# Holding back the first pieces of a layer until the last attention products are issued

## The chip, the cores and the metric

The kernel runs as one program on one core of a Trainium2 chip. The metric is the device time of one launch in microseconds (us). Three runs of the kernel before took 715.47 us in the median (715.36 to 720.8). Times are told from the start of the profiled span.

## The reference

Three blocks follow each other; q, k, v are 2 batches x 8 heads x 1152 positions x 64.

```python
q_pool = q.reshape(B, H, S // 2, 2, D).mean(axis=3)          # 576 queries a head
attn   = softmax(scale * q_pool @ k.T) ; y = attn @ v        # 16 heads
x = y as 1152 tokens x 512
h = x @ w_in                                                  # 512 x 2048
g = (a0 + a1*h + a2*h*h + a3*h**3) / (1 + |b0|*|h| + |b1|*h*h + 1e-6)
x = g @ w_out                                                 # 2048 x 512
xn = x / rms(x) * rms_g
out = (silu(xn @ w_gate) * (xn @ w_val)) @ w_out2             # 512 x 1536, 1536 x 512
```

## The kernel before, in words

**Precision.** Products of the two layers are made from pairs: a float32 number is kept as a rounded high part and the rest (`x_hi`, `x_lo`, `win_hi`, `win_lo`), and each product is three matmuls, high by high, low by high, high by low (function `three`, line 525).

**Attention.** The 16 heads are worked in 8 pairs; each pair has 9 row tiles. For a tile, TensorE makes the scores (L783), VectorE the row maximum (L812), ScalarE the exponential (L818), TensorE the transposes (L834, the last of them apart), and ScalarE or VectorE copies them out (L866, L869) into `pt`. When a head's tiles are there, 18 matmuls (9 key blocks x 2 halves, L938) make the products with the values in `av`. For a pair the row sums are inverted (L912, L913), spread by GpSimd into `rx` (L921, L923) and transposed (L985; for the last rows L971, the operation `o_rT`, copied out as `rxh` by L975). `av` is copied into `xt` (L616, L619), divided (L989 on VectorE for the first 512 columns, L994 on GpSimd for the rest), and split into `x_hi` and `x_lo` (L616 or L619, and L632).

**First layer.** Its 2048 hidden columns are 16 units of 128 (numbered from 0 here), its 1152 tokens three thirds of 384 columns. A unit's projection (L525 into `hid`) is 12 pieces: a third by one of four 128-row blocks of x, three matmuls a piece. Block 3 of the second and the last third needs the last pair of heads; the other 10 pieces of a unit don't. For units 0 and 1 (`FINE`) each piece is an operation of its own, and the rational function behind it is worked a third at a time; later units are worked whole. That function is a chain between ScalarE (ACT) and VectorE (DVE): ACT `m_u` (L1125) and `m_p` (L1128), DVE `m_q` (L1141), `m_p` twice (L1131, L1134), ACT L1144, L1147, L1153, DVE L1162, L1156, L1165, then ACT `g_hi` (L1173) and mostly GpSimd `g_lo` (L1176). L1134 is the last that reads `hid`. `hid` has two buffers, so that unit 2 waits for unit 0's L1134 and unit 3 for unit 1's. The second product (L525 into `accp`, also two buffers) sums the units of a group in PSUM; ACT (L1229) or DVE (L1231) takes each sum out into `acc`.

**Weights.** They are split on the chip as well. Those that have no room yet are made during attention and stored back to memory ("spill": ACT L175 and L215, DVE L180 and L223, GpSimd L219, the rounding L230 on ACT or L232 on GpSimd, GpSimd L236, then a DMA, L241), and fetched later (L248). `wc` has two buffers, `spill` two.

**What sets the order.** The program is recorded as operations (`Op`) with an engine (or several to choose from), a cost, a due time (`key`), the operations it waits for and its buffers. `order` walks through them with its own clock and issues, engine by engine, the ready operation that is due first. Each engine then takes its instructions strictly in that order. The due time of a unit's pieces is `key + 1960 * c` for third c; `attention` links the matmuls of the tiles and the products with values in a list `seq`, but the last head's 18 and `o_rT` stand behind no list. The first call of `order` covers attention and the projections of units 0 and 1, the second all the rest.

Of the kernel before, what the change touches and what calls it, by code (L numbers as in the profile page):

```python
# [19 lines left out]
def attention_moe_moe2_kernel(  # L20
# [425 lines left out]
    def cost(eng, n):  # L446
        return {PE: 0.45 * n, DVE: 75 + 1.04 * n, ACT: 120 + 0.834 * n, POOL: 150 + 2.13 * n}[eng]

    wop = {}
# [48 lines left out]
    xop = {}  # L498
    xread = {}

    def project_ops(w, u, key, free=(), ps=None):
        ps = ps or Buf("hid")
        if w == "in" and u in FINE or w in ("gate", "val") and u == 0:
            parts = [(c, [kk]) for c in range(NC) for kk in range(KC)]
        else:
            parts = [(c, range(KC)) for c in range(NC)]
        done = {}
        for c, kks in parts:
            before = done.setdefault(c, [])
            before.append(Op(  # L510
                PE, cost(PE, 3 * len(kks) * CW), key + 1960 * c,
                lambda c=c, kks=kks: project(w, u, c, kks),
                [wop.get((w, u)), *free, *before[-1:], *xread.get((w, u, c), ()), *(o for kk in kks for o in xop.get((c, kk), ()))],
                [ps, *wbuf[w, u]],
            ))
        return ps, done
# [72 lines left out]
    NP = len(heads) // 2  # L589
# [16 lines left out]
    NT = len(TILES)  # L606

    QW = SQ // 2
    TS = 3100
# [287 lines left out]
    def pair_ops(pr):  # L897
# [31 lines left out]
        for h in range(2):  # L929
            ab = Buf("av")  # L930
            last = None
            key = base + LAST[h] * TS + 9500
# [35 lines left out]
            if h == 1:  # L968

                def f_rT():  # L970
                    nc.tensor.transpose(e["av", 1][:, 384:512], e["rx"][:, NFULL].rearrange("p a d -> p (a d)"), ident)  # L971

                def f_rxh():
                    e["rxh"] = T("rxh", [128, 128])
                    nc.scalar.activation(e["rxh"], e["av", 1][:, 384:512], AF.Copy)  # L975

                o_rT = Op(PE, 120, key - 200, f_rT, [o_rx, last], [ab, rxb])
                o_rxh = Op(ACT, 170, key - 100, f_rxh, [o_rT], [ab, rhb])

        pb = Buf("prep")  # L980
# [35 lines left out]

    WARM = 9

    tile_pe, av_ops = {}, []
    AV2 = 5  # L1020

    def attention():
# [27 lines left out]
    early_h = {}  # L1050
# [9 lines left out]
            xop[c, kk] = [x_op[b, kk] for b in range(B) if b * SQ < (c + 1) * CW and (b + 1) * SQ > c * CW]  # L1060
    for u in FINE:
        free = [o for g in range(3) for o in lo_op[NP * NT - 2 + u, g]]
        early_h[u] = project_ops("in", u, (NP * NT + 6 * u) * TS, free)
    order(80)
    scope.pop()
    inner.close()
# [459 lines left out]
```

## Time and profile before

| | us |
|---|---|
| median of 3 runs (lowest, highest) | 715.47 (715.36, 720.8) |
| profiled execution | 718.36 |
| its span, first to last instruction | 716.6 |
| TensorE busy in the span | 689.0 (96%) |
| DVE busy, ACT busy, GpSimd (POOL) busy | 546.1, 397.6, 258.6 |
| attention's part, to the last head's products | about 277 |

The profiled execution took 1.8 us more than its span, and 2.9 us more than the median of the runs. A busy TensorE is not one at its peak: matmuls overlap, a record of 0.33 us is followed by the next after 0.17 us, and the granted clock says at which of its two levels, 1.2 or 2.4 GHz, the engine ran. The mean granted clock of the span is 0.99 of full speed.

### The profile page before, as it was taken

Reading aid. Unit: us, or ns where it says so; the run is one execution under the profiler, and the core shown is the slowest. Engines: PE = TensorE matmul, PEld = TensorE weight load, DVE = VectorE, ACT = ScalarE, POOL = GpSimd, SP = SyncE. Lnnn points to the kernel's source line nnn. Section 1 sums busy time; section 2 is a strip of 40 time slices with the busy share of each in tenths; the row PEclk is TensorE's granted clock in tenths of the full one; section 3 lists DMA queues with packets and bytes.
Section 4 is the critical chain, followed back from the end, with each engine's and each line's share of the span. In section 5 each row is a group of like instructions: output and inputs, shape, how many; then the busy total and the mean of one; then the engine's idle time right before and its main releaser. Section 6 shows DMA issues by size and latency. Waiting matters only on the chain.

```text
span 716.6 us, 13077 instructions
## 1 busy us (share of the span) xinstructions
PE 689.0 (96%) x5257; PEld 596.5 (83%) x5257; DVE 546.1 (76%) x721; ACT 397.6 (55%) x630; POOL 258.6 (36%) x240
## 2 busy tenths in 40 slices
PE   7999999999999999899999999998999999999997
PEld 6666666667666677899999999997999899989996
DVE  5599998989898885997996967957768156845844
ACT  4568776878877875977755655344334232402210
POOL 3022334656654465312221323255345033403500
PEclk9799999999999999999999999999999999999999
DMA  6443434765554535214105104000225112420103
GB/s 209 113 133 119 124 96 156 223 192 180 202 168 143 190 120 202 93 59 146 60 30 171 36 2 149 28 29 0 89 89 148 60 59 83 125 89 29 59 1 132
DMA packets 53900, 77.66 MB, mean 108 GB/s; under 512 B 6480, under 2 KB 36176, under 8 KB 53840
## 3 DMA queue, kind: packets, MB, share of 16 engines
q1 hardware_dynamic: 53840, 76.83, 33.3%
q8 instruction: 41, 0.67, 0.4%
q14 instruction: 19, 0.16, 0.1%
HBM read 62.40 MB, written 14.42 MB: 107 GB/s over the span
## 4 chain that ended last, share of the span: by engine, by line
PE 81%; DVE 12%; ACT 4%; issue 2%; DMA 0%; SPq 0%; DVEq 0%; ACTq 0%
PE hid L525 32%; PE accp L525 23%; PE hid L783 9%; PE av L938 9%; PE hid L834 5%; DVE nm L812 2%; DVE pt L869 2%; ACT p L818 2%; PE prep L732 2%; DVE acc L1324 1%; DVE xt L619 1%; DVE m_q L1141 1%; PE prep L985 1%; DVE wc L184 1%; DVE x_lo L1334 0%
## 5 line engine op out<-in xcount | busy, mean ns | idle before, releaser
L525 PE MATMUL hid<-x_hi,win_hi 128*128 128x384 f32 x480 | 162.3, 338 | 3.6 <-DVE m_p L1134 1.4
L525 PE MATMUL hid<-x_lo,win_hi 128*128 128x384 f32 x480 | 161.2, 336 | 0.6 <-DVE x_lo L1334 0.6
L525 PE MATMUL hid<-x_hi,win_lo 128*128 128x384 f32 x480 | 161.1, 336 | 0.0
L818 ACT ACTIVATE p<-hid,nm 128x1152 f32<-128x1152 f32 x72 | 87.9, 1222 | 28.2 <-DVE nm L812 28.0
L812 DVE TENSOR_REDUCE nm<-hid 128x1 f32<-128x1152 f32 x72 | 94.9, 1353 | 10.2 <-PE hid L783 8.9
L525 PEld LDWEIGHTS hid<-x_hi,win_hi 128*128 128x128 f32 x480 | 90.7, 189 | 6.7 <-issue 3.5
L783 PE MATMUL hid<-kT,qT 64*128 64x256 f32 (+3 forms) x800 | 95.2, 379 | 0.8 <-DVE pt L869 0.4
L1176 POOL TENSOR_TENSOR g_lo<-m_p,g_hi 128x1152 fp32r<-128x1152 f32 (+1 forms) x20 | 44.5, 2233 | 135.2 <-ACT g_hi L1173 96.8
L525 PEld LDWEIGHTS hid<-x_lo,win_hi 128*128 128x128 f32 x480 | 90.6, 189 | 1.8 <-DVE x_lo L1334 0.9
L525 PEld LDWEIGHTS hid<-x_hi,win_lo 128*128 128x128 f32 x480 | 90.5, 189 | 0.0
L834 PEld LDWEIGHTS hid<-ident,p 64*128 64x128 f32 x1296 | 53.6, 141 | 37.7 <-ACT p L818 12.3
L834 PE MATMUL hid<-ident,p 64*128 64x64 f32 x1296 | 68.5, 232 | 12.2 <-ACT p L818 7.0
L783 PEld LDWEIGHTS hid<-kT,qT 64*128 64x128 f32 (+1 forms) x800 | 70.5, 182 | 9.0 <-DVE pt L869 1.3
L938 PE MATMUL av<-pt,vn 128*64 128x288 f32 x576 | 76.7, 411 | 0.0
L866 ACT ACTIVATE pt<-hid 128x512 f32<-128x512 f32 (+2 forms) x145 | 59.7, 449 | 29.8 <-PE hid L834 29.3
L525 PE MATMUL accp<-g_hi,wout_hi 128*128 128x384 f32 x192 | 64.8, 337 | 3.0 <-ACT acc L1229 1.8
L525 PE MATMUL accp<-g_hi,wout_lo 128*128 128x384 f32 x192 | 64.2, 334 | 0.0
L525 PE MATMUL accp<-g_lo,wout_hi 128*128 128x384 f32 x192 | 64.2, 334 | 0.0
L938 PEld LDWEIGHTS av<-pt,vn 128*64 128x64 f32 x576 | 38.7, 136 | 27.1 <-issue 3.4
L175 ACT ACTIVATE wc<-wraw 128x512 f32<-128x512 f32 x68 | 45.4, 671 | 26.5 <-POOL win_lo L208 14.7
L869 DVE COPY pt<-hid 128x512 f32<-128x512 f32 (+1 forms) x79 | 47.6, 608 | 16.4 <-PE hid L834 14.9
L203 POOL TENSOR_SCALAR win_hi<-wc 128x512 fp32r<-128x512 f32 x22 | 15.2, 691 | 99.8 <-PE hid L525 90.8
(120 smaller groups left out, 1236.2 us busy)
## 6 DMA issues: line engine op xcount, KB each, us to landing
wraw<-in_moe_w_out_dram SPq DMA_DIRECT2D x28, 512.0 KB, 3.4
far<-spill SPq DMA_DIRECT2D x23, 512.0 KB, 3.3
wraw<-in_moe_w_in_dram SPq DMA_DIRECT2D x16, 512.0 KB, 3.8
wraw<-in_moe_w_gate_dram SPq DMA_DIRECT2D x12, 512.0 KB, 3.8
wraw<-in_moe_w_val_dram SPq DMA_DIRECT2D x12, 512.0 KB, 4.2
kn<-in_k_dram SPq DMA_DIRECT2D x16, 288.0 KB, 3.9
vn<-in_v_dram SPq DMA_DIRECT2D x16, 288.0 KB, 3.1
qn<-in_q_dram SPq DMA_DIRECT2D x16, 256.0 KB, 3.3
```

The lines of the kernel that those rows point to most:

```text
L175: nc.scalar.activation(c.bitcast(F32), wt["raw", n][:, :, 1].bitcast(F32), AF.Abs, scale=2.0**-112)
L203: eng.tensor_scalar(hi, w_float(n), 1.0, 1.0, op0=ALU.mult, op1=ALU.mult)
L525: ins = nc.tensor.matmul(dst, lhsT=a[x], rhs=b[y], start=first and i == 0 and p == 0, stop=last and i == n - 1 and p == 2,)
L732: seen(nc.tensor.transpose(ps[:, at:at + 128], src, ident))
L783: ins = nc.tensor.matmul(ps[to, j, c:c + x1 - x0], lhsT=qT[2 * pr + h][rows, c0:c0 + to.stop - to.start], rhs=kT[2 * pr + h][rows, x0:x1], ...
L812: nc.vector.tensor_reduce(out=e["nm"], in_=scores(), op=ALU.max, axis=AX.X, negate=True)
L818: nc.scalar.activation(e["p"], scores(), AF.Exp, bias=e["nm"], scale=1.0, accum_out=sums[pr][:, t:t + 1])
L834: ins = nc.tensor.transpose(ps[:, g, c:c + 64], e["p"][rows, 128 * j:128 * j + 128], ident[rows, rows])
L866: return nc.scalar.activation(to, src, AF.Copy)
L869: return nc.vector.tensor_copy(to, src)
L938: nc.tensor.matmul(e["av", h][64 * c:64 * c + 64, 0:QW], lhsT=v_tile[2 * pr + h][:, KEYS[kt], :], rhs=pt[pr, h][:, kt, c * QW:(c + 1) * QW ...
L1176: eng.tensor_sub(g_(1), p_(), g_(0).bitcast(F32))
```

## The change

All but the first two pieces of unit 0, and all pieces of unit 1, get one more operation to wait for: `o_rT` of the last pair, the matmul behind the last head's products with the values. No instruction's work changes. The wait is one in the recorded order alone (TensorE runs in order, so it needs no semaphore). Since the due times and costs are walked through anew, the places of other operations behind it move as well.

```diff
-    def project_ops(w, u, key, free=(), ps=None):
+    def project_ops(w, u, key, free=(), ps=None, behind=(), ahead=0):
...
-        for c, kks in parts:
+        for n, (c, kks) in enumerate(parts):
...
-                [wop.get((w, u)), *free, *before[-1:], *xread.get((w, u, c), ()), *(o for kk in kks for o in xop.get((c, kk), ()))],
+                [wop.get((w, u)), *free, *(behind if n >= ahead else ()), *before[-1:], *xread.get((w, u, c), ()), *(o for kk in kks for o in xop.get((c, kk), ()))],
...
                 o_rT = Op(PE, 120, key - 200, f_rT, [o_rx, last], [ab, rxb])
+                av_last[:] = [o_rT]
...
-    tile_pe, av_ops = {}, []
+    tile_pe, av_ops, av_last = {}, [], []
...
-        early_h[u] = project_ops("in", u, (NP * NT + 6 * u) * TS, free)
+        early_h[u] = project_ops("in", u, (NP * NT + 6 * u) * TS, free, None, av_last, 0 if u else 2)
```

Behind line 976 the changed kernel's lines have a number one higher (L1125 is L1126 there). Three places show what stands where now.

**TensorE (PE) at the end of attention.** Three L525 rows are one piece; L834 is the last row tile's transposes, L938 the last head's products, L971 `o_rT`. Before, the tenth piece and what follows:

```order
L525 MATMUL hid<-x_hi,win_hi 128x384
L525 MATMUL hid<-x_lo,win_hi 128x384
L525 MATMUL hid<-x_hi,win_lo 128x384
L985 MATMUL prep<-ident,rx 128x128 x4
L834 MATMUL hid<-ident,p 128x64
L938 MATMUL av<-pt,vn 64x288 x18
L971 MATMUL av<-ident,rx 128x128
```

and now, from the transposes:

```order
L834 MATMUL hid<-ident,p 128x64 x35
L525 MATMUL hid<-x_hi,win_hi 128x384
L525 MATMUL hid<-x_lo,win_hi 128x384
L525 MATMUL hid<-x_hi,win_lo 128x384
L525 MATMUL hid<-x_hi,win_hi 128x384
L525 MATMUL hid<-x_lo,win_hi 128x384
L525 MATMUL hid<-x_hi,win_lo 128x384
L986 MATMUL prep<-ident,rx 128x128 x4
L834 MATMUL hid<-ident,p 128x64
L938 MATMUL av<-pt,vn 64x288 x18
L971 MATMUL av<-ident,rx 128x128
```

Eight pieces (24 matmuls) of unit 0 moved from ahead of L985 to behind L971. Behind it stood 7 pieces of unit 1, the last 2 of unit 0 and the last 5 of unit 1; now the 10 of unit 0 stand there (the two that need the last pair last) and then the 12 of unit 1.

**ACT and GpSimd (POOL) where the last pair becomes x.** `hid_3781` is unit 0, `hid_3869` (before) is unit 1, `hid_157` the last row tile. ACT before:

```order
L175 ACTIVATE wc_3819<-wraw_3693 128x512
L215 ACTIVATE wraw_3693<-wraw_3693 128x512
L866 ACTIVATE pt_3603<-hid_157 128x128
L975 ACTIVATE rxh_3873<-av_3840 128x128
L616 ACTIVATE xt_3730<-av_3840 64x288 x2
L1125 ACTIVATE m_u_3978<-hid_3781,absb_87 128x384
L1128 ACTIVATE m_p_3983<-hid_3781,ncoef_83 128x384
L1125 ACTIVATE m_u_3987<-hid_3869,absb_87 128x384
L1128 ACTIVATE m_p_3989<-hid_3869,ncoef_83 128x384
```

ACT now:

```order
L866 ACTIVATE pt_3603<-hid_157 128x128
L175 ACTIVATE wc_3817<-wraw_3693 128x512
L215 ACTIVATE wraw_3693<-wraw_3693 128x512
L975 ACTIVATE rxh_3840<-av_3802 128x128
L616 ACTIVATE xt_3730<-av_3802 64x288 x2
L616 ACTIVATE x_hi_141<-xt_3730 128x576
L230 ACTIVATE spill_3872<-wc_3817 128x512
L1126 ACTIVATE m_u_3978<-hid_3781,absb_87 128x384
L1129 ACTIVATE m_p_3983<-hid_3781,ncoef_83 128x384
L1126 ACTIVATE m_u_3978<-hid_3781,absb_87 128x384 x2
L1129 ACTIVATE m_p_3983<-hid_3781,ncoef_83 128x384 x2
```

POOL before:

```order
L236 TENSOR_TENSOR spill<-wc,spill 128x512
L219 TENSOR_TENSOR wc<-wc,wraw 128x512
L232 TENSOR_SCALAR spill<-wc 128x512
L236 TENSOR_TENSOR spill<-wc,spill 128x512
L994 TENSOR_TENSOR xt<-xt,rxh 64x64 x2
```

POOL now:

```order
L236 TENSOR_TENSOR spill<-wc,spill 128x512
L995 TENSOR_TENSOR xt<-xt,rxh 64x64 x2
L219 TENSOR_TENSOR wc<-wc,wraw 128x512
L236 TENSOR_TENSOR spill<-wc,spill 128x512
```

The last copy of the row tile (L866) stands ahead of the last weight's two steps on ACT. `x_hi` moved from DVE (L619) to ACT, and the rounding of the last spilled weight from POOL (L232) to ACT (L230), ahead of the first operation of the rational function. POOL's part of the division stands ahead of that weight's product (L219). The chains of unit 0 and 1 are no longer mixed: all thirds of unit 0 come first.

**ACT at the first sums taken out of `accp`.** Before, from unit 1's `g_hi`; the first L1125 is unit 3's:

```order
L1173 ACTIVATE g_hi<-m_p 128x384 x3
L1125 ACTIVATE m_u<-hid,absb 128x1152
L1144 ACTIVATE m_q<-m_q 128x1152
L1229 ACTIVATE acc<-accp 128x384
L1147 ACTIVATE m_u<-m_q,b_lnq 128x1152
L1229 ACTIVATE acc<-accp 128x384 x2
L1153 ACTIVATE m_u<-m_u,b_expq 128x1152
```

and now:

```order
L1174 ACTIVATE g_hi<-m_p 128x384
L175 ACTIVATE wc<-wraw 128x512
L1145 ACTIVATE m_q<-m_q 128x1152
L1230 ACTIVATE acc<-accp 128x384
L1148 ACTIVATE m_u<-m_q,b_lnq 128x1152
L1230 ACTIVATE acc<-accp 128x384 x2
L1154 ACTIVATE m_u<-m_u,b_expq 128x1152
L1126 ACTIVATE m_u<-hid,absb 128x1152
```

Unit 3's `m_u` moved from ahead of the first sum to behind the third. From unit 10 on, the order of TensorE's work is as before; between unit 4 and unit 9 the sums stand in other portions (30 matmuls in a row behind unit 4, where 12 and 12 stood apart).

## Rows read from the trace of the kernel before

**Rows 1.** Waits of PE, 250 to 717: total us, times, longest.

```profile
PE accp L525 <- DVE acc L1231: 1.2, 2, 0.9
```

**Rows 2.** Timeline of PE: start, duration, line, form, in brackets idle time before it.

```profile
266.45 0.44 PE L525 MATMUL hid<-x_hi,win_hi 128*128 128x384 f32 x1 [0.37 <-ACT pt L866]
...
267.62 0.33 PE L525 MATMUL hid<-x_hi,win_hi 128*128 128x384 f32 x1
...
271.79 0.60 PE L985 MATMUL prep<-ident,rx 128*128 128x128 f32 x4
...
272.52 4.59 PE L938 MATMUL av<-pt,vn 128*64 128x288 f32 x36
...
277.12 0.42 PE L525 MATMUL hid<-x_hi,win_hi 128*128 128x384 f32 x1
...
284.31 0.34 PE L525 MATMUL hid<-x_hi,win_lo 128*128 128x384 f32 x1
286.06 0.41 PE L525 MATMUL hid<-x_hi,win_hi 128*128 128x384 f32 x1 [1.42 <-DVE m_p L1134]
...
292.38 0.33 PE L525 MATMUL accp<-g_hi,wout_hi 128*128 128x384 f32 x1
...
294.57 0.41 PE L525 MATMUL hid<-x_hi,win_hi 128*128 128x384 f32 x1 [0.98 <-issue]
```

**Rows 3.** The same view where the first sums are waited for.

```profile
303.88 0.45 PE L525 MATMUL accp<-g_hi,wout_hi 128*128 128x384 f32 x1 [1.76 <-ACT acc L1229]
```

**Rows 4.** Busy time by stretch: PE, PEld, DVE, ACT, POOL, granted clock, DMA.

```profile
305.00:308.50 3.50, 3.47 (x12) 3.26 (x11) 3.36 (x6) 3.50 (x5) 0.00 (x0) 0.51 0.35 121
```

**Rows 5.** The same view, other stretches.

```profile
303.90:309.00 5.10, 5.07 (x19) 4.74 (x20) 4.96 (x6) 5.10 (x6) 0.00 (x0) 0.67 0.30 102
```

**Rows 6.** The same view, the stretch behind unit 0.

```profile
285.00:294.50 9.50, 7.53 (x42) 7.23 (x42) 9.46 (x20) 9.50 (x21) 3.07 (x3) 1.00 0.47 163
```

**Rows 7.** Timeline of ACT.

```profile
277.40 0.28 ACT L975 ACTIVATE rxh<-av 128x128 f32<-128x128 f32 x1 [4.31 <-PE av L971]
...
278.55 0.58 ACT L1125 ACTIVATE m_u<-hid,absb 128x384 f32<-128x384 f32 x1
...
301.17 1.22 ACT L1125 ACTIVATE m_u<-hid,absb 128x1152 f32<-128x1152 f32 x1 [0.68 <-PE hid L525]
302.29 1.15 ACT L1144 ACTIVATE m_q<-m_q 128x1152 f32<-128x1152 f32 x1
303.34 0.48 ACT L1229 ACTIVATE acc<-accp 128x384 f32<-128x384 f32 x1
```

**Rows 8.** Timeline of POOL.

```profile
273.59 1.58 POOL L236 TENSOR_TENSOR spill<-wc,spill 128x512 fp32r<-128x512 f32 x1
...
278.46 0.71 POOL L994 TENSOR_TENSOR xt<-xt,rxh 64x64 f32<-64x64 f32 x2
```

**Rows 9.** Instructions of lines 632, 219 and 230: ns least, median, most.

```profile
L632 DVE TENSOR_TENSOR x_lo<-xt,x_hi x2: 758/1245/1732, 125.2 to 279.8; 128x576 fp32r<-128x576 f32 x2
...
L219 POOL TENSOR_TENSOR wc<-wc,wraw x23: 1281/1295/1587, 115.4 to 275.1; 128x512 f32<-128x512 f32 x23
...
L230 ACT ACTIVATE spill<-wc x2: 624/628/631, 162.2 to 212.1; 128x512 fp32r<-128x512 f32 x2
```

**Rows 10.** Timeline of DVE, the last readers of `hid` and unit 2's first.

```profile
284.79 1.13 DVE L1134 SCALAR_TENSOR_TENSOR m_p<-m_p,ncoef,hid 128x384 f32<-128x384 f32 x2
...
293.32 1.14 DVE L1134 SCALAR_TENSOR_TENSOR m_p<-m_p,ncoef,hid 128x384 f32<-128x384 f32 x2
...
294.84 0.69 DVE L184 SCALAR_TENSOR_TENSOR wc<-wraw,wc 128x512 uint32<-128x512 uint32 x1
...
299.85 1.41 DVE L1141 SCALAR_TENSOR_TENSOR m_q<-m_u,absb,hid 128x1152 f32<-128x1152 f32 x1
```

**Rows 11.** Timelines of DVE and PE where unit 8's projection begins.

```profile
343.14 1.42 DVE L1134 SCALAR_TENSOR_TENSOR m_p<-m_p,ncoef,hid 128x1152 f32<-128x1152 f32 x1
...
344.66 0.41 PE L525 MATMUL hid<-x_hi,win_hi 128*128 128x384 f32 x1
```

## The prediction

> **What bounds the kernel now.** I read the page's busy line first: TensorE (PE) is busy for 96% of the span, so a change of order can only win where PE waits or runs at its lower clock. Then PE's timeline behind attention. Three waits stand there: 1.42 us before unit 2, which needs unit 0's buffer, and 0.98 us before unit 3, which needs unit 1's [rows 2]; then 1.76 us before the third sum, because ACT had not emptied an `accp` buffer [rows 3]. Behind the third wait the stretches by clock show half of full speed, 0.51, from 305 to 308.5, which is 1.2 GHz [rows 4]; before it fell PE had stood idle for those 1.76 us [rows 3].
>
> Pieces set PE's scale: from 267.62 to 271.79 it issued 8 pieces [rows 2], 0.52 us each, 0.174 a matmul. Counted from issue to issue a wait costs about 0.25 more than its bracket: the matmul at 284.31 would have been followed at 284.48, and unit 2 started at 286.06, so 1.58, and the first product after a wait adds 0.08 [rows 2]. The clock's price: in 303.9 to 309 there are 19 matmuls in 5.1 us [rows 5], where 0.174 each would give 29, so 10 x 0.174 = 1.8 us. **Lost before, in this part:** 1.42 + 0.98 + 1.76 + 3 x 0.25 + 1.8 = 6.7 us. This is about all that the change can reach.
>
> **The products come earlier.** Eight pieces leave the place ahead of L985, so the last head's products start 8 x 0.52 = 4.17 us earlier, at 268.35 instead of 272.52 [rows 2]. Their inputs are there: the last row tile's copies are what the first piece waited for at 266.45 [rows 2], and the copy behind the last transpose no longer stands behind two weight steps on ACT. PE loses nothing, since the same pieces follow.
>
> **x comes 2.7 us earlier, not 4.2.** `rxh` moves from 277.40 [rows 7] to 273.23, and the two copies of `av` behind it end where ACT's next work began, 278.55 [rows 7], less 4.17: 274.38. But POOL's part of the division stands behind a subtraction of the spill that lasts until 275.17 [rows 8], then takes 0.7 [rows 8]: 275.84. `x_hi` is now ACT's; the nearest row is the rounding of 512 columns, 0.628 [rows 9], so about 0.7 for 576: 276.55. `x_lo` on DVE takes 0.758 or 1.732 [rows 9]. I take neither: POOL's weight product, 1.28 to 1.59 [rows 9], starts right behind the division at 275.8 and ends at 277.1 to 277.4, and the two ends of `x_lo` differ by about what is left of it. I put `x_lo` at 277.9, between 277.35 and 278.3.
>
> The Trainium skill, "SBUF — State Buffer", section "Who interferes with whom", says that a VectorE instruction with two SBUF inputs and a GpSimd instruction that reads SBUF exclude each other for a whole instruction, whoever is first. By it `x_lo` would wait for the weight product's end and then run its own 0.758, which gives 277.9 to 278.15; the sum would change by 0.25 at most, and that the larger value of [rows 9] is nearly 1 us over the smaller agrees with it.
>
> PE, free behind L971 at 277.12 - 4.17 = 272.95 [rows 2], does 8 pieces by 277.11 and then needs `x_lo`, one matmul later (277.28). **First term: a new wait of 0.7 us** (0.1 to 1.1).
>
> **The chains start only 0.7 us earlier.** ACT's first operation of the rational function started at 278.55 [rows 7]. Now the rounding of the last spilled weight stands ahead of it on ACT, in order, and it needs POOL's product (277.1 to 277.4). With 0.628 [rows 9] ACT is free at 277.85. Queued behind that rounding is everything that frees `hid`. This is the place where most of the 4.17 us is lost.
>
> **First wait gone.** From ACT's first operation to unit 0's release took 278.55 to 285.92, the end of the L1134 rows at 284.79 [rows 7, 10], with unit 1's work mixed in. Even at that length unit 0 is free at 285.2; now its thirds stand together, so earlier. PE ends unit 1 at 272.95 + 22 x 0.52 + 0.7 = 285.1. So unit 2 follows at once.
>
> **Second wait longer.** Until unit 1's release (L1134 rows at 293.32, end 294.46 [rows 10]) the same set of chain instructions has to run, 15.9 us from ACT's first. In 285 to 294.5 DVE was busy for 9.46 and ACT for 9.50 of 9.50 us [rows 6], so it can't shrink there. Unmixed, each third of unit 0 waits by turns for ACT and DVE (0.58 to 0.7 us an instruction) with no other unit to fill in; I add 0.5 (0 to 1). Release: 277.85 + 15.9 + 0.5 = 294.25, start 294.4. PE is there at 285.1 + 36 x 0.174 + 6 x 0.174 = 292.4. **2.0 us lost** (1.0 to 2.6), where 1.2 was lost before.
>
> **Third wait nearly gone.** Before, ACT's `m_u` of unit 3 stood ahead of the first sum; it waited 0.68 for PE and took 1.22, and the next, 1.15, came before the sum at 303.34 [rows 7]. That `m_u` now stands behind. Unit 2's `m_q` on DVE started 5.4 us after unit 1's release [rows 10], 1.0 of it two weight steps (the longer 0.69 [rows 10]) that now stand later: it ends at 294.25 + 4.4 + 1.4, about 300. ACT's step behind it and the sum end at 302.0, counting 0.4 for the weight step that stands between. PE has two sums done at 294.4 + 36 x 0.174 + 1.04 = 301.7: **0.3 us** (0 to 1.9). Unit 4's projection then waits for unit 2's release: **0.15 us**.
>
> **A new wait.** Behind unit 4 thirty matmuls of sums stand in a row, five sums for two buffers, and ACT empties them between operations of 1.15 to 1.3 us each. The nearest row is the wait that such a queue made, 1.76 [rows 3]. Following ACT from 302 through its next operations (two for unit 2, two for unit 3, one for unit 4, `g_hi`) I come 1.3 us late for the third of the five: **1.3 us** (0 to 1.9).
>
> **Moved DMAs.** On SP's queue the last spilled weight's store goes out about 0.7 us later than before, since POOL's last subtraction waits for ACT's rounding; the loads of two later weights stand behind a fetch instead of ahead. The fetch for unit 3 is needed at 294.4 and waits for unit 0's last piece, at about 279: covered. Without that cover a late fetch would add to the second wait.
>
> **The sum.** Lost now: 0.7 + 2.0 + 0.3 + 0.15 + 1.3 + 4 x 0.08 = 4.8. Gain 6.7 - 4.8 = 1.9, say 2.0 for the small first waits. Behind unit 10 PE's order is the same, and the later waits, 1.2 us for DVE [rows 1], I leave. The profiled execution's 718.36 becomes 716.4, its span 714.6. The runs' median stands 2.9 lower; by the same 2.0 it becomes **713.5 us**.
>
> **Rivals.** (1) *The clock falls again.* An idle stretch of 1.76 us preceded the fall [rows 3, 4], and one of 1.42 none: the stretch 285 to 294.5 has 1.00 [rows 2, 6]. My second wait is 2.0. Then PE loses 1.8 there; the waits for ACT behind it (0.3 + 0.15 + part of 1.3) absorb about 0.6. Gain 0.8: 714.7. The Trainium skill, "TensorE: Matmul & The Clock Gate", section "Why this matters for your kernels", asks for a longer idle stretch than any here before the clock falls; by that neither the old wait nor the new one would cost clock. Rows 3 and 4 speak against it. Chance 0.22.
>
> (2) *The spill does not hold ACT.* If POOL's product is done when ACT arrives, the chains start at 276.6, 1.25 earlier; the second wait is 0.75, the new one doesn't arise: lost 0.1 + 0.75 + 0.3 + 0.3 = 1.45, gain 5.2, 710.3. The order speaks against it, POOL's known lengths too. Chance 0.18.
>
> (3) *The lead is used up.* Unit 8 started 0.1 us after DVE's L1134 ended at 344.56 [rows 11], with no recorded wait: PE had no slack there. If DVE isn't ahead by then, all of the gain is a wait for DVE, and the time stays: 715.5. For it: DVE and ACT are full in [rows 6]. Against: part of DVE's idle time behind 316 was itself a wait for PE. Chance 0.12.
>
> (4) *ACT parked behind POOL, slower.* Place: the rounding ahead of ACT's first chain instruction. If POOL's three instructions ahead take their longest and the clock falls at the longer second wait, the lost time is 1.1 + 2.6 + 1.8 + 1.9 (the wait of [rows 3] stays) + 0.4 = 7.8, 1.1 over before: 716.6. It decides when ACT's first chain instruction starts later than about 278.6 with the clock falling, or 279.8 without. Against: it needs both. Chance 0.13.
>
> **How the numbers follow.** Forecast 0.35: 713.5, range for itself 712.3 to 714.8. The range over all, 710.0 to 716.6, reaches from rival 2 to rival 4 and leaves out a tail of each, about 0.2. Within 1% is 708.3 to 722.6, about what a measurement of this kernel can tell from no change. Faster than that needs all 6.7 us and some of the later waits: 0.04. Slower by 7 us has no row behind it: 0.03. Within: 0.93.
>
> **What would show it.** PE: L938 at about 268.4, a wait of about 0.7 us near 277.2 before an `x_lo` product, none before unit 2, about 2 us before unit 3 at 294.4, a short one before the third sum. ACT: its L230 ending near 277.9, and the first L1126 there; earlier is rival 2, later rival 4. Granted clock 1.00 from 294 to 310; half of it there is rival 1. Unit 8 starting about 2 us before 344.66 confirms the gain, at 344.66 it is rival 3. The forecast is wrong if the second wait is under 1 us or over 3.

## The result, and the profile after

Twelve runs of the changed kernel took 721.30 us in the median (718.37 to 723.54), twelve of the kernel before 716.89 (714.18 to 720.80). The ratio is 1.007, with a 95% interval of 1.0051 to 1.0088: slower by 3.7 to 6.3 us, where 713.5 was forecast. (The forecast counted from the 715.47 of three runs, so 1.4 us of its distance is the base's.) 721.3 lies within 1% of before, as the largest of the three chances had it, but outside the range (710.0 to 716.6) and on the other side of no change.

The profiled execution took 720.59 us, its span 718.8. Two spans can't be laid over each other here as they stand. TensorE's orders are the same up to unit 0's first piece, but that piece starts at 264.74 us, where it was 266.45 [rows 2]. The difference comes from the start of attention, where the granted clock is at 1.2 GHz for a stretch whose length varied from run to run (10.24 us before, 3.41 us here). These are rows of busy time by stretch (PE, PEld, DVE, ACT, POOL, granted clock, DMA), first of the kernel before, then of the changed one:

```profile
18.30:28.60 10.30, 9.84 (x81) 6.66 (x75) 5.39 (x6) 5.18 (x11) 0.00 (x0) 0.50 0.43 117
```

```profile
18.30:21.70 3.40, 3.23 (x47) 2.52 (x47) 1.38 (x2) 2.28 (x5) 0.00 (x0) 0.50 0.55 121
21.70:28.60 6.90, 5.89 (x75) 4.19 (x68) 5.28 (x8) 4.20 (x10) 0.00 (x0) 1.00 0.39 123
```

So from here on times with a plus sign are counted **from the first piece**: +x is x us behind it. So counted, the span ends at +450.12 before and at +454.04 now, 3.92 later, which agrees with the runs.

PE's timeline of the changed kernel where the prediction has its steps (start, duration, line, form, in brackets the idle time before it):

```profile
264.74 0.44 PE L525 MATMUL hid<-x_hi,win_hi 128*128 128x384 f32 x1 [0.37 <-ACT pt L866]
...
266.65 4.59 PE L938 MATMUL av<-pt,vn 128*64 128x288 f32 x36
...
275.50 0.34 PE L525 MATMUL hid<-x_hi,win_hi 128*128 128x384 f32 x1
275.96 0.45 PE L525 MATMUL hid<-x_lo,win_hi 128*128 128x384 f32 x1
...
292.35 0.41 PE L525 MATMUL hid<-x_hi,win_hi 128*128 128x384 f32 x1 [1.73 <-issue]
...
299.96 0.45 PE L525 MATMUL accp<-g_hi,wout_hi 128*128 128x384 f32 x1
...
311.68 0.45 PE L525 MATMUL accp<-g_hi,wout_hi 128*128 128x384 f32 x1 [0.88 <-ACT acc L1230]
...
340.14 0.34 PE L525 MATMUL accp<-g_hi,wout_lo 128*128 128x384 f32 x1
343.74 0.66 PE L525 MATMUL hid<-x_hi,win_hi 128*128 128x384 f32 x1 [3.27 <-issue]
```

Read it from the top. The last head's products start at +1.91 instead of +6.07 [rows 2], 4.16 earlier. The `x_lo` stall, the second wait, the third and the new one are there, 0.12, 1.73, under 0.3 and 0.88 us idle: together less than forecast. Then, at 343.74, stands a wait of 3.27 us that no term of the sum has. It is the start of unit 8, the place of [rows 11], where the kernel before had no wait. The view names no releaser for it; the buffer that unit 8 needs came free 0.1 us before it started (the table below). Behind it the clock is at half:

```profile
342.50:349.40 6.90, 5.66 (x18) 5.69 (x19) 5.57 (x6) 6.37 (x6) 2.03 (x1) 0.51 0.01 2
```

5.65 us of work (343.74 to 349.39) at 1.2 GHz is 2.8 us lost. Side by side, from the first piece:

| | before | changed | |
|---|---|---|---|
| ACT's first chain instruction | +12.10 | +11.24 | -0.86 |
| last reader of `hid`, unit 3, ends | +47.05 | +48.33 | +1.28 |
| the same, unit 5 | +69.00 | +67.59 | -1.41 |
| TensorE done with all ahead of unit 8 | +78.2 | +75.7 | -2.5 |
| last reader of `hid`, unit 6, ends | +78.11 | +78.90 | +0.79 |
| unit 8 starts | +78.21 | +79.00 | +0.79 |
| unit 10 starts | +112.70 | +116.56 | +3.86 |
| end of the span | +450.12 | +454.04 | +3.92 |

TensorE did come to unit 8 2.5 us ahead, more than the 2.0 forecast. Unit 6's buffer came free 0.79 later than before. So 0.79 is lost at the start of unit 8, some 2.8 by the clock behind it (an estimate, the next section measures it), and from unit 10 on nothing more.

Why was the buffer later, when unit 5's was 1.41 earlier? DVE's timeline from unit 5's last reader to unit 6's, in the kernel before:

```profile
334.04 1.41 DVE L1134 SCALAR_TENSOR_TENSOR m_p<-m_p,ncoef,hid 128x1152 f32<-128x1152 f32 x1
336.56 1.42 DVE L1162 SCALAR_TENSOR_TENSOR m_p<-m_p,ncoef,m_u 128x1152 f32<-128x1152 f32 x1 [1.11 <-ACT m_u L1153]
337.90 1.35 DVE L1156 SCALAR_TENSOR_TENSOR m_q<-m_q,m_u 128x1152 f32<-128x1152 f32 x1
339.16 1.41 DVE L1141 SCALAR_TENSOR_TENSOR m_q<-m_u,absb,hid 128x1152 f32<-128x1152 f32 x1
340.49 1.35 DVE L1165 SCALAR_TENSOR_TENSOR m_p<-m_q,m_p 128x1152 f32<-128x1152 f32 x1
341.76 1.35 DVE L1131 TENSOR_TENSOR m_p<-m_p,hid 128x1152 f32<-128x1152 f32 x1
```

and in the changed kernel:

```profile
330.91 1.42 DVE L1135 SCALAR_TENSOR_TENSOR m_p<-m_p,ncoef,hid 128x1152 f32<-128x1152 f32 x1
333.08 2.79 DVE L1163 SCALAR_TENSOR_TENSOR m_p<-m_p,ncoef,m_u 128x1152 f32<-128x1152 f32 x1 [0.75 <-ACT m_u L1154]
335.79 1.35 DVE L1157 SCALAR_TENSOR_TENSOR m_q<-m_q,m_u 128x1152 f32<-128x1152 f32 x1
337.06 1.40 DVE L1142 SCALAR_TENSOR_TENSOR m_q<-m_u,absb,hid 128x1152 f32<-128x1152 f32 x1
338.38 1.34 DVE L1166 SCALAR_TENSOR_TENSOR m_p<-m_q,m_p 128x1152 f32<-128x1152 f32 x1
339.65 1.34 DVE L1132 TENSOR_TENSOR m_p<-m_p,hid 128x1152 f32<-128x1152 f32 x1
340.91 1.40 DVE L1142 SCALAR_TENSOR_TENSOR m_q<-m_u,absb,hid 128x1152 f32<-128x1152 f32 x1
342.24 1.40 DVE L1135 SCALAR_TENSOR_TENSOR m_p<-m_p,ncoef,hid 128x1152 f32<-128x1152 f32 x1
```

The last L1134 of before is in [rows 11]. From end to end it is 9.11 us before and 11.31 now. Two things are new: a second L1142, 1.40, which is unit 7's `m_q` and stands ahead of the reader that TensorE waits for, and L1163, which takes 2.79 instead of 1.42. POOL's subtraction for unit 4 runs beside it:

```profile
331.97 2.68 POOL L1177 TENSOR_TENSOR g_lo<-m_p,g_hi 128x1152 fp32r<-128x1152 f32 x1 [6.93 <-ACT g_hi L1174]
```

In the kernel before, the same subtraction ran from 332.42 to 335.11 and was done 1.45 us before L1162 began:

```profile
332.42 2.69 POOL L1176 TENSOR_TENSOR g_lo<-m_p,g_hi 128x1152 fp32r<-128x1152 f32 x1 [5.50 <-ACT g_hi L1173]
```

Counted from the first piece, the step now comes 1.77 us earlier and the subtraction 1.26 us later, so that they meet. The Trainium skill, "SBUF — State Buffer", section "Who interferes with whom", says that a DVE instruction with two inputs in SBUF (here `m_p` and `m_u`) and a GpSimd one that reads SBUF exclude each other for a whole instruction. Here the trace agrees within 0.2 us: POOL ends at 334.65, and L1163, of 1.41 us alone, ends 1.22 us behind it, at 335.87.

### The profile page after: what moved, and what is told of

Its sections match the earlier page's. It is cut to its first block, busy times and chain, and to the rows that moved or that the text cites. A ratio compares the mean times of both kernels' runs of the same rounds, so it can differ in the third digit from the quotient of the medians.

```text
span 718.8 us, 13083 instructions
## 1 busy us (share of the span) xinstructions
PE 687.5 (96%) x5257; PEld 596.0 (83%) x5257; DVE 547.0 (76%) x720; ACT 398.3 (55%) x632; POOL 257.2 (36%) x239
## 2 busy tenths in 40 slices
DMA packets 53900, 77.66 MB, mean 108 GB/s; under 512 B 6480, under 2 KB 36176, under 8 KB 53840
## 4 chain that ended last, share of the span: by engine, by line
PE 75%; DVE 15%; ACT 6%; issue 3%; POOL 1%; DMA 0%; SPq 0%; DVEq 0%; POOLq 0%
PE hid L525 29%; PE accp L525 21%; PE hid L783 8%; PE av L938 8%; PE hid L834 5%; DVE nm L812 3%; ACT p L818 3%; DVE pt L869 2%; PE prep L732 2%; DVE m_q L1142 1%; ACT m_p L1129 1%; DVE acc L1325 1%; DVE xt L619 1%; ACT m_u L1126 1%; DVE wc L184 1%
## 5 line engine op out<-in xcount | busy, mean ns | idle before, releaser
L525 PE MATMUL hid<-x_hi,win_hi 128*128 128x384 f32 x480 | 162.5, 339 | 6.3 <-issue 5.2
L525 PE MATMUL hid<-x_lo,win_hi 128*128 128x384 f32 x480 | 161.8, 337 | 0.8 <-DVE x_lo L1335 0.6
L525 PE MATMUL hid<-x_hi,win_lo 128*128 128x384 f32 x480 | 161.3, 336 | 0.0
L525 PEld LDWEIGHTS hid<-x_hi,win_hi 128*128 128x128 f32 x480 | 90.9, 189 | 9.1 <-issue 6.2
L783 PE MATMUL hid<-kT,qT 64*128 64x256 f32 (+3 forms) x800 | 93.5, 374 | 0.9 <-DVE pt L869 0.4
L525 PEld LDWEIGHTS hid<-x_lo,win_hi 128*128 128x128 f32 x480 | 90.8, 189 | 2.2 <-DVE x_lo L1335 0.9
L525 PEld LDWEIGHTS hid<-x_hi,win_lo 128*128 128x128 f32 x480 | 90.8, 189 | 0.0
L834 PEld LDWEIGHTS hid<-ident,p 64*128 64x128 f32 x1296 | 53.4, 140 | 37.8 <-ACT p L818 13.7
L834 PE MATMUL hid<-ident,p 64*128 64x64 f32 x1296 | 68.1, 231 | 13.1 <-ACT p L818 8.1
L938 PE MATMUL av<-pt,vn 128*64 128x288 f32 x576 | 76.7, 411 | 0.0
L866 ACT ACTIVATE pt<-hid 128x512 f32<-128x512 f32 (+2 forms) x145 | 59.7, 449 | 29.2 <-PE hid L834 28.7
L525 PE MATMUL accp<-g_hi,wout_hi 128*128 128x384 f32 x192 | 65.2, 339 | 2.4 <-DVE acc L1232 1.5
L525 PE MATMUL accp<-g_hi,wout_lo 128*128 128x384 f32 x192 | 64.4, 335 | 0.0
L525 PE MATMUL accp<-g_lo,wout_hi 128*128 128x384 f32 x192 | 64.4, 335 | 0.0
L938 PEld LDWEIGHTS av<-pt,vn 128*64 128x64 f32 x576 | 38.6, 136 | 27.2 <-issue 3.4
```

The lines of the kernel that those rows point to most:

```text
L525: ins = nc.tensor.matmul(dst, lhsT=a[x], rhs=b[y], start=first and i == 0 and p == 0, stop=last and i == n - 1 and p == 2,)
L783: ins = nc.tensor.matmul(ps[to, j, c:c + x1 - x0], lhsT=qT[2 * pr + h][rows, c0:c0 + to.stop - to.start], rhs=kT[2 * pr + h][rows, x0:x1], ...
L834: ins = nc.tensor.transpose(ps[:, g, c:c + 64], e["p"][rows, 128 * j:128 * j + 128], ident[rows, rows])
L866: return nc.scalar.activation(to, src, AF.Copy)
L938: nc.tensor.matmul(e["av", h][64 * c:64 * c + 64, 0:QW], lhsT=v_tile[2 * pr + h][:, KEYS[kt], :], rhs=pt[pr, h][:, kt, c * QW:(c + 1) * QW ...
```

## The experiments

The theories were **A**: the chains between ACT and DVE set when unit 8 can start, so TensorE's lead can't be kept, and the wait costs clock on top. **B**: the moved pieces gain as forecast, and the new order of the second part (all behind units 0 and 1) does the harm. C and E came later and stand in the expectations. Ratios are to runs of the kernel before on the same chip, with 95% intervals. In most of these kernels the lines have numbers 10 to 12 higher.

### The price of the clock

```diff
+        if (w, u, c) == ("in", 8, 0):
+            for _ in range(50):
+                nc.tensor.matmul(spare[0][:, CW:512], lhsT=x_hi[:, 0, 0:128], rhs=x_hi[:, 0, 0:128], start=False, stop=False)
         hidden_tile(w, u)()
```

This stands ahead of unit 8's first piece; the second kernel has 24 instead of 50. `spare` is the `accp` tile of the sum that is under way; its last 128 columns are used by nobody.

> The changed kernel with 50 idle matmuls of 128 columns (about 2.9 us) ahead of unit 8's first piece, into columns that nobody reads. They take nothing from the work, since TensorE waits there for 3.27 us. If the half clock behind that wait comes from the idle time: unit 8 starts within 0.3 us of where it did, the granted clock stays at 1.00 from 342 to 350, and the time falls by 3.4 us, to about 718. If the clock falls for another reason: 721.3 us as in the changed kernel, or up to 0.3 more.

720.81 us, 1.0062 (1.0042 to 1.0082). The clock stayed at 1.00, but the fifty took 5.5 us, so that unit 8 started at +81.3, 2.3 late. The end was +453.70, 0.34 earlier than without them. The idle work had the wrong size, so once more:

> The changed kernel with 24 idle matmuls ahead of unit 8. Fifty of them took 5.5 us, 0.11 each, and put off unit 8 by 2.3 us; 24 take 2.6 and end inside the wait of 3.27 us. Unit 8 starts 79.0 us behind the first piece as without them. If the half clock behind the wait (5.65 us of work, 2.8 us lost) is the price of the idle time, it is gone and the time is 718.5 us; if the clock falls all the same, 721.3.

719.29 us, 1.0035 (1.0014 to 1.0057). Unit 8 starts at +79.0 as before the edit; the rows show PE around it and the stretch behind:

```profile
340.76 2.79 PE L579 MATMUL accp<-x_hi 128*128 128x128 f32 x24
344.16 0.41 PE L535 MATMUL hid<-x_hi,win_hi 128*128 128x384 f32 x1 [0.61 <-issue]
```

```profile
344.10:351.00 6.90, 6.84 (x40) 6.88 (x40) 6.38 (x6) 5.87 (x6) 0.87 (x1) 1.00 0.00 0
```

These 6.9 us, from unit 8's start on, hold 40 recorded matmuls. In the changed kernel the same stretch has 25:

```profile
343.70:350.60 6.90, 6.86 (x25) 6.89 (x26) 5.63 (x5) 5.17 (x5) 0.83 (x1) 0.59 0.01 2
```

Unit 10 starts at +114.37 instead of +116.56, the end comes 2.23 earlier. So the idle time did bring the clock down, and that is 2.2 of the 3.9 us; the rest of the 2.8 turned up as waits behind it (the 36 matmuls of sums at +86.3 took 6.7 us instead of 6.2).

### Which part of the order

A table puts the order of one kernel into the other: each number is an operation and its engine, in the order of the walk. Both kernels have the same operations, so the second parts can be exchanged.

```diff
+    FORCED = {
+        0: [6584, 6588, 5576, 6740, 6744, 6600, 5604, 6592, 6604, 6756, 6636, 6596, 6640, 5484,
...
+            if table:
+                n = table.pop()
+                op = next(o for o in ready if o.at == n // 4)
+                op.eng, op.cost, op.fn = op.ways[n % 4]
+                picks = [(begin(op), op)]
             t, op = min(picks, key=lambda e: (e[0], e[1].at))
```

> The changed kernel's order to the end of attention and of units 0 and 1, and behind it, for everything, the order of the kernel before. Theory A (the chains between ACT and DVE set when unit 8 can start, so TensorE's lead can't be kept): ACT's first chain instruction is only 0.86 us earlier than before, counted from the first piece, so unit 8 starts 0 to 1 us earlier than before, behind a wait of 2 to 3.5 us; 716 to 717 us if the clock holds, 719 to 720 if it falls as in the changed kernel. Theory B (the moved pieces gain as forecast, and the new order of the second part does the harm): with the old second part the gain stays, 713.5 to 715.5 us, and no wait over 1.5 us stands before unit 8.

717.89 us, 1.0009 (0.9988 to 1.0029): no difference from before that the runs can tell. The end is +449.69, unit 8 starts at +77.8 with no wait over 0.6. The lead is gone much earlier than A had it: unit 2 now waits 1.81 us for unit 0's buffer and starts 1.02 us later than before. PE there, and the stretch behind its 1.76 us wait before the third sum:

```profile
285.72 0.41 PE L535 MATMUL hid<-x_hi,win_hi 128*128 128x384 f32 x1 [1.81 <-DVE m_p L1145]
```

```profile
303.40:308.50 5.10, 4.89 (x27) 4.60 (x28) 5.02 (x7) 5.10 (x7) 0.00 (x0) 1.00 0.31 105
```

Here the clock held behind that wait, where the profiled execution of the kernel before fell to half behind the same one [rows 3, 4]. So the 0.43 by which the end is earlier by the profiles is no gain of the moved pieces. B's gain of 2 us didn't come; the time is 0.9 over A's 717, and not by A's wait at unit 8.

> The reverse: the order of the kernel before to the end of units 0 and 1, and behind it the changed kernel's order. Theory A: the new second part costs what it puts ahead of unit 6's release on DVE, one instruction of 1.4 us (unit 7's m_q); TensorE has no lead to lose, so a wait of 1 to 2 us before unit 8 and a clock that holds: 717.5 to 719 us. Theory B: the second part's order is the whole loss, and without the front's gain it is larger: 721 to 723 us.

724.06 us, 1.0091 (1.0062 to 1.012): slower than the changed kernel even. B's figure is nearer. The two long waits, each followed by the half clock:

```profile
296.70 0.41 PE L535 MATMUL hid<-x_hi,win_hi 128*128 128x384 f32 x1 [2.76 <-issue]
...
349.31 0.66 PE L535 MATMUL hid<-x_hi,win_hi 128*128 128x384 f32 x1 [3.24 <-issue]
```

The two kernels settle where the harm sits. From unit 5's last reader of `hid` to unit 6's it is 9.11 us with the old second part, whichever front stands ahead of it (+69.00 to +78.11, +68.55 to +77.66), and 11.31 with the new one (+67.59 to +78.90, +71.13 to +82.44). The 2.2 us belong to the new order of the second part. And the front alone gains nothing while that part stays as it was. Neither theory is right by itself.

### Do the chains set it?

Here the first part's order is put in as a table too, with one entry 5377 instead of the changed kernel's 5376: the last spilled weight's rounding goes to GpSimd, as before. All else stands as in the changed kernel. The entry with its neighbours:

```python
5412, 5420, 4293, 5424, 5377, 5428, 5380, 5416,
```

> The changed kernel with one instruction on another engine: the rounding of the last spilled weight is GpSimd's again, so that it no longer stands ahead of ACT's first chain instruction. All other orders are the changed kernel's. Theory A (the chains set when unit 8 can start): ACT's first chain instruction comes 0.6 to 1.3 us earlier (11.24 us behind the first piece now), unit 8 starts up to 1.3 us earlier than 79.0 us behind the first piece, and the wait before it shrinks by as much; 717 to 720.5 us. Theory B (the order behind unit 1 is what costs, wherever the chains begin): the first chain instruction moves, unit 8 and the time do not: 721 us.

718.93 us, 1.0032 (1.0015 to 1.0048). ACT's first chain instruction comes at +10.11, 1.13 earlier, right behind `x_hi`. The rounding ahead of it in the changed kernel, then ACT in this one:

```profile
275.32 0.63 ACT L230 ACTIVATE spill<-wc 128x512 fp32r<-128x512 f32 x1 [0.69 <-POOL wc L219]
```

```profile
273.28 0.69 ACT L627 ACTIVATE x_hi<-xt 128x576 fp32r<-128x576 f32 x1 [1.49 <-POOL xt L1006]
273.99 0.58 ACT L1137 ACTIVATE m_u<-hid,absb 128x384 f32<-128x384 f32 x1
```

Every release of `hid` up to unit 6 is 0.7 earlier (unit 3 at +47.60, unit 6 at +78.17), and so is unit 8. TensorE's wait there stays (3.23), since it too arrives earlier. Here the half clock lasted 3.41 us instead of 6.83, and the end is 1.90 earlier, of which 0.73 is unit 8's earlier start. B expected unit 8 and the time to stay, and both moved: the chains do set when unit 8 starts.

### What in the chains

In these cuts of the table's one long line, the first is the changed kernel's order.

```diff
-        7964, 7144, 7244, 7188, 7148, 7176, 7232, 7280,
+        7964, 7144, 7176, 7244, 7188, 7148, 7232, 7280,
```

7176 is unit 6's last reader of `hid`, 7244 unit 7's `m_q`, both on DVE.

> The changed kernel with two neighbours on DVE exchanged: unit 6's last reader of hid stands ahead of unit 7's m_q (1.40 us) instead of behind it. Theory A: unit 8 starts 1.4 us earlier, the wait before it is 1.9 us instead of 3.27; 719.9 us if the clock still falls there, about 716.5 if it holds. Theory B: the same 1.4 us at most, since the other moved sums stay: 719.9.

720.38 us, 1.0043 (1.0022 to 1.0065). Unit 8 starts at +78.0, 1.0 earlier instead of 1.4, behind a wait of 2.04; the half clock is there, 3.41 us long. The end is 0.94 earlier.

```profile
343.29 0.41 PE L535 MATMUL hid<-x_hi,win_hi 128*128 128x384 f32 x1 [2.04 <-issue]
```

That is near A with the clock still falling; B gave the same 719.9, so the time doesn't tell the two apart. What it shows is that this one neighbour on DVE held unit 8 by 1.0 us.

Next the six weight steps (5584 to 5620) are moved down the table, behind unit 6's last reader, and an entry whose turn has come but which isn't ready is passed over for the time being:

```diff
-        7964, 7144, 7244, 7188, 7148, 7176, 7232, 7280,
+        7964, 7144, 7244, 7188, 7148, 7176, 5584, 5588, 5612, 5592, 5616, 5620, 7232, 7280,
...
-                op = next(o for o in ready if o.at == n // 4)
+                at = {o.at: o for o in ready if open_(o)}
+                n = next(n for n in reversed(table) if n // 4 in at)
```

> The changed kernel with six instructions on DVE moved: the steps of two weights that stood between unit 2's and unit 3's chains (0.4 to 0.7 us each, 3.5 us together) stand behind unit 6's last reader of hid. Theory A: DVE is the engine that sets unit 8, so unit 6's buffer comes free 1.0 us (these steps lie partly in a wait for ACT) to 3.5 us earlier than 78.9 us behind the first piece, the wait before unit 8 falls from 3.27 to under 2.3 us, and the time by 1 to 5 us, to 716 to 720. Theory B: DVE has idle time enough in that stretch, unit 8 starts within 0.5 us of where it did: 721 us.

722.03 us, 1.0067 (1.0044 to 1.0091). Unit 6's buffer comes free at +78.80, where it was. **This refutes A in the form it had there**: taking 3.5 us of work off DVE in that stretch gives nothing, so the sum of DVE's work isn't what sets unit 8. Moved behind the release, the steps cost a wait later (unit 10 at +117.79).

Both together, and the same exchange for unit 3 (6984 is its last reader, 7052 unit 4's `m_q`):

```diff
+        7856, 6952, 6984, 7052,
...
+        7964, 7144, 7176, 5584, 5588, 5612, 5592, 5616, 5620, 7244, 7188, 7148, 7232, 7280,
```

> The changed kernel with three moves on DVE alone: unit 3's last reader of hid ahead of unit 4's m_q, unit 6's ahead of unit 7's m_q, and the six weight steps behind unit 6's last reader. Moving the weight steps alone left unit 6's release where it was (78.8 us behind the first piece), exchanging the pair of unit 6 alone made it 1.0 us earlier. Theory A, as the runs leave it (the place of single chain steps in DVE's fixed order decides, not the sum of DVE's work): together they free unit 3's buffer 2 us earlier than 48.3 and unit 6's 2 to 3.5 us earlier, the wait before unit 8 falls under 1.5 us and the clock holds; 715.5 to 718.5 us. Theory E (ACT's steps set the pace whatever DVE's order is): unit 6's release stays between 77.5 and 78.5, the wait before unit 8 at about 2 us; 720 us.

726.22 us, 1.0136 (1.0114 to 1.0157), the slowest of all, far from A's time and from E's. Unit 3's buffer was free 1.9 earlier, unit 6's only 1.3 (+77.58), and the wait before unit 8 was 2.03, both as E had it. The weight steps then stood in DVE's order ahead of everything that the sums needed. DVE, then PE:

```profile
344.41 2.47 DVE L180 TENSOR_SCALAR wc<-wc 128x512 uint32<-128x512 uint32 x1
346.91 0.69 DVE L184 SCALAR_TENSOR_TENSOR wc<-wraw,wc 128x512 uint32<-128x512 uint32 x1
...
349.17 0.69 DVE L190 SCALAR_TENSOR_TENSOR wc<-wraw,wc 128x512 uint32<-128x512 uint32 x1
```

```profile
357.10 0.44 PE L537 MATMUL accp<-g_hi,wout_hi 128*128 128x384 f32 x1 [3.40 <-DVE acc L1244]
```

What was left between the two readers in this kernel was the long L1163. So the last of this set takes POOL's subtraction away there:

```diff
             def f_lo(eng=nc.gpsimd):
+                if u == 4:
+                    return eng.memset(g_(1).bitcast(F32), 0.0)
                 eng.tensor_sub(g_(1), p_(), g_(0).bitcast(F32))
```

> after_release_first once more (unit 6's last reader of hid ahead of unit 7's m_q on DVE), and unit 4's GpSimd subtraction (2.68 us, L1177) is a write of zeros that reads nothing; so the low part of unit 4's g is left out of the sums. Between unit 5's and unit 6's last readers DVE's step L1163 took 2.78 us beside that subtraction, where 1.41 is usual. Theory A (DVE's order and GpSimd's subtraction beside it set unit 6's release): L1163 takes 1.41 there, and unit 8 starts 1.0 to 1.4 us earlier than in after_release_first, where it was 78.0 us behind the first piece; its wait falls from 2.04 to about 0.9 us, the clock holds, and the time is 2.5 to 3.2 us below after_release_first's 720.4: 717 to 718 us. Theory E (ACT's steps set the pace): L1163 is shorter, but DVE waits for ACT by as much behind it; unit 8 at 77.7 to 78.2, 720 us.

718.67 us, 1.0043 (1.0024 to 1.0062). DVE, where the step is L1173, and PE at unit 8:

```profile
334.13 1.42 DVE L1173 SCALAR_TENSOR_TENSOR m_p<-m_p,ncoef,m_u 128x1152 f32<-128x1152 f32 x1 [0.74 <-ACT m_u L1164]
...
340.71 1.42 DVE L1145 SCALAR_TENSOR_TENSOR m_p<-m_p,ncoef,hid 128x1152 f32<-128x1152 f32 x1
```

```profile
342.23 0.41 PE L535 MATMUL hid<-x_hi,win_hi 128*128 128x384 f32 x1 [0.67 <-issue]
```

The writes of zeros don't wait for ACT and ran 7 us earlier (326.05 to 327.12), so that nothing of POOL lies beside the step. It takes 1.42, unit 6's buffer is free at +76.56, 1.37 earlier than in after_release_first, unit 8 starts at +76.7, and the clock holds. A's mechanism is shown, and E is out for this place. A's time is not reached: the end is +451.67, 1.43 earlier instead of 2.5 to 3.2, and the ratio didn't move. Unit 8 now starts 1.5 us ahead of the kernel before, and unit 10 still 1.5 behind it (+114.23). A wait of 1.48 us for DVE's sum (L1244) stands at 356.22. The next POOL subtraction lies beside DVE's next L1173, which takes 3.48 us there, and the sum stands behind it. Removing the two troubles moves TensorE on to the next pair of them.

### A rule that orders the chains as a whole

The walk takes among the ready operations the one due first, but only among those that can start as early as the earliest. An operation right behind its forerunner on DVE counts as ready 127 ns later, so a step of a later unit, or of a weight that isn't due for long, went ahead of it. One number changes that in the second part:

```diff
-        order(0)
+        order(130)
```

> The changed kernel with one number changed: among the operations that could start within 130 ns of the earliest the one due first is taken, in place of the earliest alone, in everything behind units 0 and 1. So a chain's own next step on DVE stands ahead of a later unit's step and of weight steps that are due much later. Theory A: unit 8 then starts 2 to 4 us earlier than 79.0 us behind the first piece, without a wait over 1.7 us before it and with the clock at 1.00 there; 713 to 716 us, below the kernel before. Theory C (the moved pieces can gain nothing, since the chains start no earlier): no better than the kernel before, 716 to 718 us.

713.00 us, **0.995 (0.9931 to 0.9968)**: faster than both kernels. DVE from unit 5's last reader to unit 6's, and PE at unit 8:

```profile
329.21 1.42 DVE L1135 SCALAR_TENSOR_TENSOR m_p<-m_p,ncoef,hid 128x1152 f32<-128x1152 f32 x1
331.55 1.42 DVE L1142 SCALAR_TENSOR_TENSOR m_q<-m_u,absb,hid 128x1152 f32<-128x1152 f32 x1 [0.92 <-ACT m_u L1126]
332.88 1.41 DVE L1163 SCALAR_TENSOR_TENSOR m_p<-m_p,ncoef,m_u 128x1152 f32<-128x1152 f32 x1
334.21 1.35 DVE L1157 SCALAR_TENSOR_TENSOR m_q<-m_q,m_u 128x1152 f32<-128x1152 f32 x1
335.60 1.36 DVE L1166 SCALAR_TENSOR_TENSOR m_p<-m_q,m_p 128x1152 f32<-128x1152 f32 x1
336.87 1.35 DVE L1132 TENSOR_TENSOR m_p<-m_p,hid 128x1152 f32<-128x1152 f32 x1
338.25 1.42 DVE L1135 SCALAR_TENSOR_TENSOR m_p<-m_p,ncoef,hid 128x1152 f32<-128x1152 f32 x1
```

```profile
339.77 0.41 PE L525 MATMUL hid<-x_hi,win_hi 128*128 128x384 f32 x1 [0.25 <-issue]
```

No step of unit 7 stands in between, L1163 has its 1.41, since the subtraction (327.87 to 330.57) ended before it; 9.03 us from end to end. Unit 8 starts at +75.2, 3.8 earlier than in the changed kernel and 3.0 earlier than before, and the clock is full, all as A had it. Is that the rule, or the moved pieces?

> The kernel before with the one number of after_order_130 and without the moved pieces. after_order_130 was 2.2 us ahead of the kernel before where unit 10 starts, and 4.3 at the end. If the gain up to unit 10 is the moved pieces' (their lead, kept by the new order) and the rest the number's: unit 10 starts 0 to 1 us from where the kernel before has it (112.7 us behind the first piece), and the time is 714 to 716 us. If all is the number's: unit 10 at about 110.5, 713 us. If the number needs the moved pieces: 717 us or more.

716.13 us, 0.9996 (0.9977 to 1.0015): the rule without the moved pieces makes no difference that the runs can tell. Unit 10 starts at +113.22, 0.5 from where the kernel before has it, as the first of the three cases had it, and 2.77 later than with the moved pieces. A part of the 2.77 is clock: behind unit 2's wait it fell here, and with the moved pieces it held.

```profile
287.20 0.55 PE L525 MATMUL hid<-x_hi,win_hi 128*128 128x384 f32 x1 [2.24 <-DVE m_p L1134]
```

Behind unit 10 the gain is the number's alone: from there to the end it is 337.42 us in the kernel before and 337.48 in the changed one, and with the number 335.42 without the moved pieces and 335.38 with them.

| ratio to before (median us) | `order(0)` | `order(130)` |
|---|---|---|
| pieces as before | 1 (716.9) | 0.9996 (716.1) |
| pieces moved | 1.007 (721.3) | 0.995 (713.0) |

The same move costs 0.7% under one rule and gives 0.5% under the other.

With the weight's rounding taken off ACT as well:

```diff
+            if f is s_hi and n == SPILL[-1]:
+                ways = ways[1:]
```

> after_order_130 with the last spilled weight's rounding on GpSimd, so that ACT's first chain instruction doesn't wait for it. Where that was done in the changed kernel alone, the chains and unit 8 came 0.7 us earlier. If the chains still set the pace, the wait before unit 3 (1.70 us) and the one before the first sums behind it (0.92) shrink by 0.7 together at least: 712 to 712.7 us. If TensorE is the bound there now, 713 us as without it.

712.63 us, 0.9957 (0.994 to 0.9974): not to be told from 713.0. The wait before unit 3 is 0.96 instead of 1.70, and the one of 0.92 is gone; by the profile the end is 0.5 earlier.

## Why the prediction was wrong

**The step that failed** is the end of the sum: "Behind unit 10 PE's order is the same, and the later waits, 1.2 us for DVE [rows 1], I leave". The waits were worked out one by one up to the new one behind unit 4, at +46.9. For the 66 us from there to unit 10 the sum has no term, though the section on the change said that the sums stand in other portions there. In its place the runs showed a wait of 3.27 us before unit 8, whose buffer came free 0.79 later than before, and a half clock behind it that cost 2.2 us. The rows of that place ([rows 11]) were read for rival 3 alone.

- *The products come earlier*: right, 4.16 us.
- *The new `x_lo` wait*, 0.7 (0.1 to 1.1): 0.12 idle, 0.29 counted from issue to issue. `x_lo` took 1.24 us, between the two lengths of [rows 9], and ended 0.61 us behind POOL's weight product.
- *The chains start only 0.7 us earlier*: 0.86. Right, and for the reason given: with the rounding elsewhere it is 1.13 more.
- *First wait gone*: right. *Second wait* 2.0: 1.73 idle, 1.89 from issue to issue, as the forecast counts. *Third* 0.3: 0.23. *New wait* 1.3: 0.88 idle, about 1.0 from issue to issue. All within their bounds, all a little high. The sign of being wrong that the forecast named, a second wait under 1 us or over 3, didn't show: the trouble came later.
- *The clock's price*, 1.8, was counted as lost in every run, but it was read from one execution. front_after_rest_before and before_order_130 had the same 1.76 us wait at full clock, and some runs of the kernel before had a mean granted clock of 1.00 (714.2 us), where the profiled one had 0.99. So a part of the 6.7 us was there to win in some runs only.
- So TensorE was 2.5 us ahead at unit 8, and the forecast's own test, "about 2 us before 344.66", looked only at TensorE. What it asked for had to be there twice: TensorE early *and* unit 6's buffer early. [Rows 11] showed no slack between the two before: the L1134 ended at 344.56 and unit 8 started at 344.66.
- *Rival 3* (0.12) named the place. It took the release as unmoved and the lead as merely lost, 715.5. The release moved back by 0.79, since the new order put a step ahead of it and brought a DVE step beside POOL's subtraction; and behind an idle time of 3.27 us the clock cost 2.2 us. Its chance was too low: [rows 6] showed ACT and DVE full, and a unit's six DVE steps take 8.0 us in a row (336.56 to 344.56 before), about the pace at which TensorE asked for buffers (unit 7 at +69.1, unit 8 at +78.2).
- *Rivals 1 and 4* had a fall of the clock, but behind the second wait. Behind that one (1.73) it stayed at full speed. Rival 2's early chains didn't come.

That the harm came from the order behind the moved pieces, and not from the pieces, is shown by the exchange of the second parts and by the two-by-two table. That the 2.2 us in DVE's stretch are unit 7's step and POOL's subtraction is shown by after_release_first and after_no_sub, which together made the release 2.3 earlier. What stays open: with both troubles gone the changed kernel started unit 10 still 1.5 us behind the kernel before, by the next pair of them; and which of the many moves in after_order_130 carry its gain wasn't taken apart, neither up to unit 10 nor behind it, where the number alone gives 2.0 us.

## What to carry to other kernels

Where an order is worked out anew by a walk with costs, a change at one place is a change everywhere behind it: follow the waits as far as the order differs, not as far as the edit reaches. A lead of the busiest engine is worth only what the releases that it waits for gain as well, so put both beside each other at each buffer's release. And an idle time made by a lost lead can cost about as much by the clock behind it (2.2 us here) as the lead was to bring (2.0).

## What the hardware showed that was not expected

- **DVE beside POOL.** In all the traces together, the step of L1163 took 1.40 to 1.42 us where it began outside POOL's subtraction (136 times), and 1.50 to 3.85 us where it began inside (60 times); it then ended 1.21 or 1.22 us behind the subtraction each time. The kernel before has such meetings as well (2.80 us at 345.30), but none between unit 5's and unit 6's last readers.
- **The clock.** Behind attention it went to 1.2 GHz at idle stretches of 2.03, 2.04, 2.24, 2.76, 3.23, 3.24 and twice 3.27 us. It held behind one of 3.40 us, in after_dve_clear. Of twelve between 1.69 and 1.81 us it fell at one (1.76, before) and held at the others, two of them 1.76 as well. So the length of one idle stretch alone doesn't say whether it falls. The stretch at half lasted 6.83 us at the changed kernel's wait of 3.27 us, and 3.41 us at the same 3.27 in after_weights_later and at 3.23 in round_on_pool.
- **Small matmuls.** 128 columns took 0.11 us each in a row, where 384 columns take 0.174: filling a wait by the columns' share put unit 8 off by 2.3 us.
